# Windowed attention and a hard-swish feed-forward: all attention matmuls in 64x64 tiles of the array, in one stretch for each pair of heads

## The chip, the cores and the metric

The kernel runs on one core of a Trainium2 chip. The metric is device time in microseconds (us), the median of several runs. One more execution is taken with the hardware profiler; its trace has the start and the duration of the instructions on each engine: PE (TensorE matmuls), PEld (TensorE weight loads), DVE (VectorE), ACT (ScalarE), POOL (GpSimd, which here also issues the loads) and SP (which issues the other transfers).

## The reference

Causal attention in a window of 64 tokens, then a feed-forward layer with a hard-swish. Inputs and output are float32.

```python
def _attn_ref(q, k, v):                      # q, k, v: (8, 8, 576, 64), batch, heads, seq, head_dim
    window = 64
    scale = 1.0 / np.sqrt(D)
    scores = scale * np.matmul(q, k.transpose(0, 1, 3, 2))
    rel = pos[:, None] - pos[None, :]
    mask = (rel >= 0) & (rel < window)
    scores = np.where(mask, scores, -1000000000.0)
    attn = np.exp(scores - np.max(scores, axis=-1, keepdims=True))
    attn = attn / (np.sum(attn, axis=-1, keepdims=True) + 1e-09)
    return np.matmul(attn, v)

def _moe_ref(x, w_in, w_out):                # x: (4608, 512), w_in: (512, 2048), w_out: (2048, 512)
    h = x @ w_in
    relu6 = np.clip(h + 3.0, 0.0, 6.0)
    return (h * relu6 / 6.0) @ w_out

def reference(...):
    attn_out = _attn_ref(q, k, v)
    x = attn_out.transpose(0, 2, 1, 3).reshape(B * S, H * D)
    return _moe_ref(x, w_in, w_out)
```

## The kernel before

**Sizes.** There are 8 batches of 576 tokens and 8 heads of 64. Two heads make a pair, so a batch has 4 pairs, and the 32 pairs are numbered t = 4b + g. The feed-forward part is cut into 9 blocks of 512 tokens. A block has 16 first units and 16 second units. A first unit is four matmuls of 128x128 by 512 columns into one bank of PSUM (hT, L364), a relu on ACT (L369) and a multiply on DVE into gT (L370). A second unit is four matmuls (L388); every fourth one is followed by a copy on ACT (L394) and a store. Units stand in a queue, and `weave(n)` records the next n.

**Order.** The order on each engine is the order in which the Python code records the instructions (a manual schedule). Each engine works through its own list in order and waits at an instruction until what it needs is done. The rings of buffers decide when a tile can be written again. PSUM has 8 banks: two for `ps_o` (one tile of two banks), three for `ps_t`, two for `ps_h` (the hT tiles) and one for `ps_acc`.

**Attention of one pair.** q and k of a batch are loaded with 6 tokens on each of 96 partitions, and v with one token a partition, 64 numbers of one head at a time (L97, L108). A second copy of v, moved by 64 tokens, is made by transfers (`shift`, Vs<-Vn). `permute` (L170) reorders q and k on DVE, `t_k` and `t_q` turn them with 6 matmuls each (L178), and KT is copied out on DVE (L214), QZ in two halves on ACT (L203). QZ holds each head with zeros in the other head's rows, so that one matmul of 128 rows gives the scores of both heads. `s_` and `sl_` make the scores of 9 windows with 9 matmuls of 128x128 (L246) and take the exponential on ACT (L258, L268); `m_` multiplies by the mask on POOL (L277, L281). `pv` is 20 matmuls of 128x64 (L303), whose 65th column is the sum of the weights, then one reciprocal and one multiply on DVE (L312, L313). `x_` writes the result transposed into xT by a transfer, or by 5 matmuls and a copy in the first two batches.

**A step** (`step(t, units)`, L602) spreads the work of three pairs between the units: pv(t), some units, scores of t+1, some units, the turn of k for t+2, some units, the turn of q for t+2, some units. In batches 3 to 7 a step has 8 units, second and first in turn.

**The start.** The loads stand in one queue of POOL: q and k of batch 0 pair by pair, v of batch 0, w_in, q and k and v of batch 1, w_out. In batches 0 and 1 the mask is added by a matmul ahead of each score matmul (L223). `shift` of batch 0 is done by DVE and ACT copies (L586 to L590), and pv of pairs 1 and 3 writes into two tiles of `ps_h`, so that two pairs are in work at a time. `tiles_of_zeros` (L519) runs matmuls on zeros in several tile shapes while PE waits for v.

Of the kernel before, what the change touches and what calls it, by code (L numbers as in the profile page):

```python
# [10 lines left out]
F32 = mybir.dt.float32  # L11
# [16 lines left out]
R = 6  # L28
VC = 72
# [3 lines left out]
def kernel(  # L33
# [14 lines left out]
    SP = S // R  # L48
    NW = S // W
    NM = (S + P - 1) // P  # L50
    NFC = FF // P
    TB = 512
    XR = 5 * TB
    NTB = NT // TB
    assert D * H == DM and S % W == 0 and SP * R == S and SP <= P and NT % TB == 0
    assert NW == 2 * (NM - 1) + 1 and NG * P == DM
# [3 lines left out]
    stage = ctx.enter_context(tc.tile_pool(name="stage", bufs=4))  # L60
    permp = ctx.enter_context(tc.tile_pool(name="permp", bufs=1))
# [3 lines left out]
    osbp = ctx.enter_context(tc.tile_pool(name="osb", bufs=3))  # L65
    ps_o = ctx.enter_context(tc.tile_pool(name="ps_o", bufs=1, space=PSUM))
    ps_t = ctx.enter_context(tc.tile_pool(name="ps_t", bufs=3, space=PSUM))
    ps_h = ctx.enter_context(tc.tile_pool(name="ps_h", bufs=2, space=PSUM))
    ps_acc = ctx.enter_context(tc.tile_pool(name="ps_acc", bufs=1, space=PSUM))

    fb = ctx.enter_context(tc.tile_pool(name="fb", bufs=1))
# [8 lines left out]
    xT = consts.tile([P, NG, XR], BF16, name="xT")  # L80
    KT = ring(4, [P, W + S], BF16, "KT")
    QZ = ring(4, [P, 2, S], BF16, "QZ")
    Vn = ring(2, [P, NM, H, VC], BF16, "Vn")
    Vs = ring(2, [P, NM, H, VC], BF16, "Vs")
    Pz = ring(4, [P, 2, NM - 1, 2, W], BF16, "Pz")
    Pl = ring(4, [P, 2, P], BF16, "Pl")


    def load_qk(b, pairs=(NG,), first=0):
        if first:  # L90
            tiles = staged[b]
        else:
            tiles = [stage.tile([SP, H, R * D], BF16, name=name, tag="qk") for name in ("qs", "ks")]
        h = 2 * first
        for n in pairs:
            for t, src in zip(tiles, (q, k)):
                nc.gpsimd.dma_start(  # L97
                    out=t[:, h : h + 2 * n, :],
                    in_=src[b, h : h + 2 * n].rearrange("h (p r) d -> p h (r d)", r=R),
                )  # L100
            h += 2 * n
        return tiles

    def load_v(b, blocks=range(NM)):
        vn = Vn[b % 2]
        for m in blocks:
            n = min(P, S - m * P)
            nc.gpsimd.dma_start(  # L108
                out=vn[:n, m, :, 0:D],
                in_=v[b, :, m * P : m * P + n, :].rearrange("h s d -> s h d"),  # L110
            )

    def shift(b, blocks=(0, NM), heads=(0, H), move=nc.sync.dma_start):

        vn, vs = Vn[b % 2], Vs[b % 2]
        hs = slice(*heads)
        m0, m1 = blocks
# [609 lines left out]
```

## Time and profile before

| what | value |
|---|---|
| runs, median (lowest to highest) | 334.14 us (333.66 to 334.91) |
| the profiled execution | 334.16 us, of which the trace spans 332.4 us |
| granted TensorE clock, mean | 0.998 |
| first pv (pair 0) | 17.87 us |
| first matmul of the feed-forward part | 23.42 us |
| pv of pair 12, the first step of batch 3 | 89.18 us |
| last matmul | ends about 326.5 us |

The span is what the trace covers; the remaining 1.8 us of that execution lie around it. Idle time of an engine matters only where another engine that sets the end waits for it. Matmuls overlap in the trace, so their pace is read from the starts of neighbours and not from the duration of one.

### The profile page before, as it was taken

The page shows a single profiled execution, that of the slowest core. Times are in us where ns is not written, and L with a number is a line of the kernel's source. Part 1 is how long each engine was busy: PE and PEld are TensorE (multiplying, and loading weights), DVE is VectorE, ACT ScalarE, POOL GpSimd, SP SyncE. Part 2 cuts the span into 40 slices and gives each one's busy share as a digit, 9 for nine tenths or more (in the row PEclk, how much of TensorE's full clock was granted, in tenths as well). Part 3 has the DMA queues.
Part 4 walks back from the last instruction along what each step waited for, and adds up shares of the span by engine and source line. Part 5 has one row for each costly group of instructions (what it writes and reads, how often), then busy time and mean ns, then how long its engine had stood idle before and what let it go on. Part 6 is the DMA issues. An engine that isn't in the chain of part 4 may idle for free.

```text
span 332.4 us, 6785 instructions
## 1 busy us (share of the span) xinstructions
PE 314.7 (95%) x2661; PEld 166.4 (50%) x2707; DVE 181.8 (55%) x337; ACT 201.8 (61%) x345; POOL 120.7 (36%) x153
## 2 busy tenths in 40 slices
PE   7987899989999999999999999999999999999992
PEld 3753555545555555555555555555544444444441
DVE  6777665676665655565556555655544533444300
ACT  2867881868766666666666666666664444454420
POOL 8954514444558335733564356533330000000000
PEclk9999999999999999999999999999999999999999
DMA  6999999995359954995499539951211100001011
GB/s 84 164 207 179 234 206 181 198 160 130 76 71 179 115 125 72 177 103 134 76 189 107 131 60 198 115 133 51 55 51 51 66 32 32 34 32 63 35 66 69
DMA packets 76600, 36.89 MB, mean 111 GB/s; under 512 B 55056, under 2 KB 70480, under 8 KB 76560
## 3 DMA queue, kind: packets, MB, share of 16 engines
q0 software_dynamic: 53840, 18.35, 50.1%
q1 hardware_dynamic: 22720, 18.02, 22.6%
q8 instruction: 23, 0.38, 0.5%
q14 instruction: 17, 0.14, 0.1%
HBM read 36.70 MB, written 9.44 MB: 139 GB/s over the span
## 4 chain that ended last, share of the span: by engine, by line
PE 78%; DMA 9%; POOL 5%; ACT 3%; issue 2%; another core or an unknown queue 1%; DVE 1%; POOLq 0%; ACTq 0%
PE acc L388 35%; PE hT L364 32%; DMA qs<-in_q_dram 4%; PE o L303 3%; PE tp L178 3%; PE sc L246 3%; DMA Vs<-Vn 3%; DMA ks<-in_k_dram 2%; POOL Vn L108 1%; ACT t L369 1%; POOL ks L97 1%; ACT QZ L203 1%; POOL qs L97 1%; POOL Pz L277 1%
## 5 line engine op out<-in xcount | busy, mean ns | idle before, releaser
L370 DVE SCALAR_TENSOR_TENSOR gT<-t,hT 128x512 bf16<-128x512 bf16 x140 | 96.1, 687 | 119.0 <-ACT t L369 117.9
L388 PE MATMUL acc<-wout,gT 128*128 128x512 bf16 x561 | 143.7, 379 | 0.8 <-issue 0.2
L364 PE MATMUL hT<-xT,win 128*128 128x512 bf16 x532 | 140.9, 379 | 1.8 <-DVE gT L370 0.2
L369 ACT ACTIVATE t<-hT,half_const 128x512 bf16<-128x512 f32 x140 | 96.3, 688 | 57.6 <-PE hT L364 53.6
L277 POOL TENSOR_TENSOR Pz<-e,mask 128x512 bf16<-128x512 bf16 x48 | 54.3, 1150 | 100.3 <-ACT e L258 100.3
L388 PEld LDWEIGHTS <-gT 128*128 128x128 bf16 x576 | 54.2, 98 | 62.5 <-issue 0.2
L364 PEld LDWEIGHTS <-win 128*128 128x128 bf16 x576 | 52.4, 98 | 50.3 <-issue 0.5
L203 ACT COPY QZ<-tp 64x576 bf16<-64x576 bf16 x60 | 37.9, 632 | 17.9 <-PE tp L178 11.2
L258 ACT ACTIVATE e<-sc 128x512 bf16<-128x512 f32 x48 | 26.1, 595 | 21.7 <-PE sc L246 21.7
L108 POOL DMA_DIRECT2D Vn<-in_v_dram x40 | 34.2, 872 | 11.8 <-DMA wout<-in_moe_w_out_dram 6.0
L394 ACT COPY osb<-acc 128x512 f32<-128x512 f32 x36 | 20.9, 581 | 18.3 <-PE acc L388 15.3
L313 DVE TENSOR_TENSOR opg<-o,recs 128x640 bf16<-128x640 f32 x30 | 24.7, 825 | 1.0
L214 DVE COPY KT<-tp 128x576 bf16<-128x576 bf16 x32 | 24.0, 751 | 1.1 <-PE tp L190 1.0
L246 PEld LDWEIGHTS <-KT 128*128 128x128 bf16 x216 | 14.8, 98 | 7.7
L303 PEld LDWEIGHTS <-Pz 128*64 128x64 bf16 x512 | 12.1, 110 | 12.9 <-issue 11.1
L303 PE MATMUL o<-Vs,Pz 128*64 128x65 bf16 x240 | 14.6, 198 | 1.1 <-DMA Vs<-Vn 0.8
L178 PE MATMUL tp<-ident,kp 96*128 96x96 bf16 x168 | 11.8, 206 | 3.7 <-DVE kp L170 3.5
L246 PE MATMUL sc<-QZ,KT 128*128 128x128 bf16 x192 | 14.7, 219 | 0.1
L303 PE MATMUL o<-Vn,Pz 128*64 128x65 bf16 x240 | 14.6, 198 | 0.0
L178 PEld LDWEIGHTS <-kp 96*128 96x128 bf16 x168 | 9.2, 97 | 8.7 <-DVE kp L170 5.0
L97 POOL DMA_DIRECT2D qs<-in_q_dram x12 | 9.0, 749 | 10.3 <-DVE recs L312 4.7
L178 PEld LDWEIGHTS <-qp 96*128 96x128 bf16 x168 | 9.9, 97 | 5.2
(75 smaller groups left out, 201.7 us busy)
## 6 DMA issues: line engine op xcount, KB each, us to landing
out_dram<-osb SPq DMA_DIRECT2D x36, 256.0 KB, 2.0
Vn<-in_v_dram POOLq DMA_DIRECT2D x32, 128.0 KB, 5.7
qs<-in_q_dram POOLq DMA_DIRECT2D x6, 576.0 KB, 7.0
ks<-in_k_dram POOLq DMA_DIRECT2D x6, 576.0 KB, 10.3
Vs<-Vn SPq DMA_DIRECT2D x6, 360.0 KB, 4.1
wout<-in_moe_w_out_dram POOLq DMA_DIRECT2D x2, 1024.0 KB, 15.7
Vs<-Vn SPq DMA_DIRECT2D x6, 288.0 KB, 4.7
win<-in_moe_w_in_dram POOLq DMA_DIRECT2D x2, 512.0 KB, 7.1
```

Source lines behind the costliest of these rows:

```text
L108: nc.gpsimd.dma_start(out=vn[:n, m, :, 0:D], in_=v[b, :, m * P : m * P + n, :].rearrange("h s d -> s h d"),)
L178: nc.tensor.transpose(out=tp[:, r, :], in_=src[:, r, 2 * g : 2 * g + 2, :].rearrange("p h d -> p (h d)"), identity=ident[:SP, :SP],)
L203: (nc.vector.tensor_copy if h and t in on_vector else nc.scalar.copy)(out=QZ[t % 4][h * D : (h + 1) * D, h, :].rearrange("q (p r) -> q p r ...
L246: nc.tensor.matmul(sc[:, i], lhsT=kt[:, w * W : w * W + P], rhs=qz[:, :, w * W : (w + 1) * W], start=True, stop=True,)
L258: nc.scalar.activation(out=e[:, 2 * i : 2 * i + 2].rearrange("p m a h w -> p (m a h w)"), in_=sc[:].rearrange("p m h w -> p (m h w)"), fun ...
L277: eng.tensor_tensor(out=Pz[t % 4][:, :, :, a].rearrange("p h m w -> p m h w"), in0=e[:, :, a], in1=mk, op=MULT,)
L303: nc.tensor.matmul(om[a * W : (a + 1) * W], lhsT=pl[:, h, a * W : (a + 1) * W] if last else pz[:, h, m, a, :], rhs=(vn if a and not last e ...
L313: nc.vector.tensor_tensor(out=opg[:, :, hs].rearrange("p m h d -> p h m d"), in0=ov[:, :, :, 0:D], in1=rec.unsqueeze(3).to_broadcast([P, 2 ...
L364: nc.tensor.matmul(hT, lhsT=win16[:, g, fc * P : (fc + 1) * P], rhs=xT[:, g, t0 : t0 + TB], start=(g == 0), stop=(g == NG - 1),)
L369: nc.scalar.activation(out=t1[:], in_=hT, func=RELU, bias=half_const[:], scale=1.0 / 6.0)
L370: nc.vector.scalar_tensor_tensor(out=gT[:, fc, :], in0=t1[:], scalar=1.0, in1=hT, op0=MIN, op1=MULT)
L388: nc.tensor.matmul(acc[:], lhsT=gT[:, fc, ts * P : (ts + 1) * P], rhs=wout16[:, fc, :], start=(fc == 0), stop=(fc == NFC - 1),)
```

## The change

Every attention matmul is now made in a quarter of the array: 64 rows by 64 columns.

- Queries and keys are loaded with 9 tokens on each of 64 partitions, k on partitions 0 to 63 and q on 64 to 127 of one tile. `turn` makes 36 matmuls for a pair (9 tokens x 2 heads x q and k), all into one two-bank tile `tp` of `ps_t`, which has now one such tile; `turned` copies KT out on DVE and QT on ACT. `permute`, the zeros of QZ and the copies they need are gone.
- Scores: `s_first` makes the first window with 4 matmuls into unused columns of the tile `tp` of the pair after (its host), and `s_rest` the other 8 windows with 32 matmuls into two tiles of `ps_h`. Each key window is split into even and odd tokens, since v is loaded with two tokens a partition. `ps_h` has 3 tiles, for hT and for these.
- `pv` is 48 matmuls; `pv_out` has five DVE instructions in place of two.
- `x_` uses two transfers a pair in all batches but the first, where it uses matmuls. xT holds all 4608 tokens.
- `group(t, n)` records everything of the attention in one stretch, and all n units after it.
- The start: v of batch 0 is loaded before pair 3's q and k, there are four mask tiles, `shift(0)` is a transfer, and pv, pv_out and x_ of the four pairs of batch 0 stand one after the other with one `ps_o` tile. `tiles_of_zeros` is gone.
- In the last blocks every other accumulator is in `ps_o`, not `ps_t`.

```diff
-R = 6
-VC = 72
+R = 9
+VW = 144
+VO = 8
+OC = D + 2
...
-    ps_t = ctx.enter_context(tc.tile_pool(name="ps_t", bufs=3, space=PSUM))
-    ps_h = ctx.enter_context(tc.tile_pool(name="ps_h", bufs=2, space=PSUM))
+    ps_t = ctx.enter_context(tc.tile_pool(name="ps_t", bufs=1, space=PSUM))
+    ps_h = ctx.enter_context(tc.tile_pool(name="ps_h", bufs=3, space=PSUM))
...
+    def load_v(b, blocks=(0, 1, 2)):
+        for m in blocks:
+            to = Vn[b % 2][:, m] if m < 2 else Vs[b % 2][3 * P // 4 : P, 1]
+            n = 2 * to.shape[0]
+            nc.gpsimd.dma_start(
+                out=to[:, :, VO : VO + P],
+                in_=v[b, :, 2 * P * m : 2 * P * m + n, :].rearrange("h (p r) d -> p h (r d)", r=2),
+            )
+    def shift(b):
+        vn, vs = Vn[b % 2], Vs[b % 2]
+        nc.sync.dma_start(out=vs[0 : P - 32], in_=vn[32:P])
+        nc.sync.dma_start(out=vs[P - 32 : P, 0], in_=vn[0:32, 1])
...
+    def turn(t, pool=None):
+        b, g = divmod(t, NG)
+        tp = (pool or ps_t).tile([P, 2, 8 * P], BF16, name="tp", tag="o" if pool is ps_o else "tp")
+        hosts[t] = tp
+        for r in range(R):
+            for h in range(2):
+                for z in range(2):
+                    nc.tensor.transpose(
+                        out=tp[halves[h], z, r * W : (r + 1) * W],
+                        in_=staged[b][halves[z], 2 * g + h, r * D : (r + 1) * D],
+                        identity=ident[halves[z], halves[z]],
+                    )
+    def turned(t):
+        tp = hosts[t]
+        for z, (to, copy) in enumerate(((KT, nc.vector.tensor_copy), (QT, nc.scalar.copy))):
+            copy(
+                out=to[t % 4][:].rearrange("q (p r) -> q p r", r=R),
+                in_=tp[:, z, 0:S].rearrange("q (r p) -> q p r", p=W),
+            )
...
+    def keys(t, h, k0, r):
+        return KT[t % 4][halves[h], k0 + r : k0 + P : 2]
...
+    def s_first(t, host, masked):
+        s = hosts[host][0:D, :, 6 * P : 8 * P].bitcast(F32).rearrange("p h (r w) -> p h r w", w=W)
+        if masked:
+            for h in range(2):
+                off(s[:, h], halves[h], off_first)
+        for r in range(2):
+            for h in range(2):
+                nc.tensor.matmul(
+                    s[:, h, r], lhsT=keys(t, h, 0, r), rhs=QT[t % 4][halves[h], 0:W],
+                    start=not masked, stop=not masked or r == 1,
+                )
+        return s
+    def s_first_exp(t, s, masked):
+        to = P0[t % 4] if masked else work.tile([D, 2, 2, W], BF16, name="e0")
+        nc.scalar.activation(
+            out=to[:].rearrange("p h r w -> p h (r w)"), in_=s.rearrange("p h r w -> p h (r w)"),
+            func=EXP, scale=scale,
+        )
+        if not masked:
+            nc.gpsimd.tensor_tensor(
+                out=P0[t % 4][:], in0=to[:], in1=first[0:D].unsqueeze(1).to_broadcast([D, 2, 2, W]), op=MULT
+            )
+    def s_rest(t, masked):
+        ss = [ps_h.tile([P, 2, 2, 2, W], F32, name="s", tag="bk") for _ in range(2)]
+        for c in range(2):
+            for m in range(2):
+                if masked:
+                    for h in range(2):
+                        for i in range(2):
+                            nc.tensor.matmul(
+                                ss[h][halves[i], c, m], lhsT=ident[halves[h], halves[h]],
+                                rhs=off_band[halves[h]], start=True, stop=False,
+                            )
+                for r in range(2):
+                    for h in range(2):
+                        for i in range(2):
+                            w = 4 * m + 2 * i + 1 + c
+                            nc.tensor.matmul(
+                                ss[h][halves[i], c, m, r], lhsT=keys(t, h, W * (w - 1), r),
+                                rhs=QT[t % 4][halves[h], w * W : (w + 1) * W],
+                                start=not masked, stop=not masked or r == 1,
+                            )
+        return ss
+    def s_rest_exp(t, ss, masked):
+        for h in range(2):
+            to = Pw[t % 4][:, h] if masked else work.tile([P, 2, 2, 2, W], BF16, name="e", tag=f"e{h}")[:]
+            nc.scalar.activation(
+                out=to.rearrange("p c m r w -> p (c m r w)"),
+                in_=ss[h][:].rearrange("p c m r w -> p (c m r w)"), func=EXP, scale=scale,
+            )
+            if not masked:
+                nc.gpsimd.tensor_tensor(
+                    out=Pw[t % 4][:, h].rearrange("p c m r w -> p (c m) (r w)"),
+                    in0=to.rearrange("p c m r w -> p (c m) (r w)"),
+                    in1=band[:].rearrange("p r w -> p (r w)").unsqueeze(1).to_broadcast([P, 4, P]), op=MULT,
+                )
...
+    def pv(t):
+        b, g = divmod(t, NG)
+        o = ps_o.tile([P, 2, 512], F32, name="o", tag="o")
+        os_[t] = o
+        for m in range(2):
+            for h in range(2):
+                for r in range(2):
+                    c0 = (2 + 2 * m + h) * OC + r
+                    v0 = VO - 1 + r * (D + 1)
+                    for c in range(2):
+                        for i in range(2):
+                            nc.tensor.matmul(
+                                o[halves[c], i, c0 : c0 + D + 1], lhsT=Pw[t % 4][halves[i], h, c, m, r],
+                                rhs=(Vs if c else Vn)[b % 2][halves[i], m, 2 * g + h, v0 : v0 + D + 1],
+                                start=(r == 0), stop=(r == 1), skip_group_check=True,
+                            )
+        for h in range(2):
+            for r in range(2):
+                c0, v0 = h * OC + r, VO - 1 + r * (D + 1)
+                for c in range(2):
+                    for i in range(2):
+                        nc.tensor.matmul(
+                            o[halves[c], i, c0 : c0 + D + 1],
+                            lhsT=Pw[t % 4][halves[i], h, 0, 0, r] if i else P0[t % 4][:, h, r],
+                            rhs=Vn[b % 2][halves[i], 0, 2 * g + h, v0 : v0 + D + 1],
+                            start=(r == 0), stop=(r == 1), skip_group_check=True,
+                        )
+    def pv_out(t):
+        o = os_.pop(t)
+        ov = o[:, :, 0 : 6 * OC].rearrange("p i (s c) -> p i s c", c=OC)
+        sums = work.tile([P, 2, 6], F32, name="sums")
+        nc.vector.reduce_sum(out=sums[:], in_=ov[:, :, :, 0 : OC : OC - 1], axis=mybir.AxisListType.X)
+        rec = recs[:, t]
+        nc.vector.reciprocal(out=rec, in_=sums[:])
+        opg = work.tile([P, 2, 2, 2, D], BF16, name="opg")
+        opg0 = work.tile([D, 2, D], BF16, name="opg0")
+        nc.vector.tensor_tensor(
+            out=opg0[:], in0=ov[0:D, 0, 0:2, 1 : D + 1],
+            in1=rec[0:D, 0, 0:2].unsqueeze(2).to_broadcast([D, 2, D]), op=MULT,
+        )
+        for i in range(2):
+            nc.vector.tensor_tensor(
+                out=opg[:, :, i], in0=ov[:, i, 2:6, 1 : D + 1].rearrange("p (m h) d -> p m h d", h=2),
+                in1=rec[:, i, 2:6].rearrange("p (m h) -> p m h", h=2).unsqueeze(3).to_broadcast([P, 2, 2, D]),
+                op=MULT,
+            )
+        opgs[t] = opg, opg0
...
+    def x_(t, on_pe=False):
+        b, g = divmod(t, NG)
+        opg, opg0 = opgs.pop(t)
+        x0 = b * S
+        if not on_pe:
+            nc.sync.dma_start_transpose(
+                out=xT[:, g, x0 + W : x0 + S].rearrange("p (m q) -> p m q", q=P),
+                in_=opg[:].rearrange("p m i h d -> p (m i h d)"),
+            )
+            nc.sync.dma_start_transpose(
+                out=xT[:, g, x0 : x0 + W].unsqueeze(1), in_=opg0[:].rearrange("p h d -> p (h d)")
+            )
+            return
...
+    nc.vector.memset(zeros[:], 0.0)
+    staged = {0: load_qk(0, pairs=(1,))}
+    nc.gpsimd.memset(ident[:], 0.0)
+    nc.gpsimd.affine_select(
+        out=ident[:], in_=ident[:], pattern=[[-1, P]], compare_op=mybir.AluOpType.not_equal,
+        fill=1.0, base=0, channel_multiplier=1,
+    )
+    load_qk(0, pairs=(1,), first=1)
+    windows(off_band, off_first, 0.0, -BIG)
+    load_qk(0, pairs=(1,), first=2)
+    load_v(0)
+    load_qk(0, pairs=(1,), first=3)
+    for t in Vn + Vs:
+        nc.vector.memset(t[:, :, :, 0:VO], 1.0)
+        nc.vector.memset(t[:, :, :, VO + P : VW], 1.0)
+    for i in range(3):
+        load_w_in(i)
+    windows(band, first, 1.0, 0.0)
+    staged[1] = load_qk(1, pairs=(2,))
+    load_v(1)
+    load_qk(1, pairs=(NG - 2,), first=2)
+    for i in range(2):
+        load_w_out(i)
+    shift(0)
+    nc.vector.memset(ones[:], 1.0)
+    nc.vector.memset(half_const[:], 0.5)
...
+    warm(12)
+    turn(0)
+    turned(0)
+    turn(1, ps_o)
+    turned(1)
+    s_masked(0)
+    turn(2)
+    turned(2)
+    s_masked(1)
+    turn(3, ps_o)
+    turned(3)
+    s_masked(2)
+    s_masked(3)
+    pv(0)
+    pv_out(0)
+    x_(0, True)
+    for g in range(1, NG):
+        pv(g)
+        pv_out(g)
+        warm(2)
+        x_(g, True)
+    def group(t, n):
+        masked = t + 1 < 2 * NG
+        if t >= NG:
+            pv(t)
+        if t + 2 < T:
+            turn(t + 2)
+        if NG <= t + 1 < T:
+            host = t + 2
+            if host >= T:
+                hosts[host] = ps_t.tile([P, 2, 8 * P], BF16, name="tp", tag="tp")
+            s = s_first(t + 1, host, masked)
+            s_first_exp(t + 1, s, masked)
+            ss = s_rest(t + 1, masked)
+        if t >= NG:
+            pv_out(t)
+        if t + 2 < T:
+            turned(t + 2)
+        if NG <= t + 1 < T:
+            s_rest_exp(t + 1, ss, masked)
+        if t >= NG:
+            x_(t)
+        weave(n)
...
+    queue_block(0)
+    weave(3)
+    group(NG - 2, 2)
+    group(NG - 1, 2)
+    moe.extend(left[:10])
+    del left[:10]
+    for t in range(NG, T):
+        b, g = divmod(t, NG)
+        if b == 1:
+            if g == 0:
+                shift(1)
+                staged[2] = load_qk(2)
+            if g == 1:
+                load_v(2)
+            if g == 2:
+                shift(2)
+                staged[3] = load_qk(3)
+            n = -(-len(moe) // (NG - g))
+        else:
+            if g == 0:
+                queue_block(b - 1)
+                if 3 <= b < B - 1:
+                    staged[b + 1] = load_qk(b + 1)
+            if g == 1 and b < B - 1:
+                load_v(b + 1)
+            if g == 2 and b + 1 < B:
+                shift(b + 1)
+            n = -(-len(moe) // (NG - g))
+        group(t, n)
+    late[0] = True
```

## The prediction

> **What bounds the kernel now.** I read the page's busy times and its chain that ended last first, then the timeline of one step of PE.
>
> ```profile
> PE 314.7 (95%) x2661; PEld 166.4 (50%) x2707; DVE 181.8 (55%) x337; ACT 201.8 (61%) x345; POOL 120.7 (36%) x153
> ...
> PE 78%; DMA 9%; POOL 5%; ACT 3%; issue 2%; another core or an unknown queue 1%; DVE 1%; POOLq 0%; ACTq 0%
> ```
>
> PE is busy for 95% and makes 78% of the chain. Whether it is dense is read from one step of batch 3 (columns: start, duration, engine, line, operation):
>
> ```profile
> 106.45 0.22 PE L303 MATMUL o<-Vs,Pz 128*64 128x65 bf16 x1
> ...
> 106.89 1.04 PE L388 MATMUL acc<-wout,gT 128*128 128x512 bf16 x4
> 107.77 0.61 PE L246 MATMUL sc<-QZ,KT 128*128 128x128 bf16 x8
> 108.21 1.03 PE L364 MATMUL hT<-xT,win 128*128 128x512 bf16 x4
> ...
> 109.94 0.22 PE L246 MATMUL sl<-QZ,KT 128*128 128x128 bf16 x1
> 110.00 0.42 PE L178 MATMUL tp<-ident,kp 96*128 96x96 bf16 x6
> 110.25 1.03 PE L364 MATMUL hT<-xT,win 128*128 128x512 bf16 x3
> ...
> 111.98 0.42 PE L178 MATMUL tp<-ident,qp 96*128 96x96 bf16 x6
> 112.24 1.03 PE L364 MATMUL hT<-xT,win 128*128 128x512 bf16 x4
> ...
> 114.92 0.22 PE L303 MATMUL o<-Vs,Pz 128*64 128x65 bf16 x1
> ```
>
> From pv (106.45) to the next pv (114.92) are 8.47 us, and each start follows the one before it without a hole. A unit takes 0.863 us (263.55 to 264.41 below), so 8 units take 6.91; the remaining 1.56 are pv 0.44, scores 0.44 and 0.06, turns 0.25 and 0.26, the rest changes of tile shape (pv begins 0.09 after the unit before it). So here PE alone sets the end, and all else is hidden. Before batch 3 that is not so: from the first unit (23.42) to pv of pair 12 (89.18) are 65.8 us, in which 48 units take 41.4.
>
> **What one stretch of the change costs PE.** The trace has 64x64 tiles, on zeros:
>
> ```profile
> 15.98 0.22 PE L534 MATMUL za<-zeros 64*64 64x64 bf16 x2
> 15.99 0.22 PE L534 MATMUL zb<-zeros 64*64 64x64 bf16 x2
> ...
> 16.16 0.20 PE L534 MATMUL za<-zeros 64*64 64x64 bf16 x2
> 16.29 0.40 PE L526 MATMUL za<-zeros 128*128 128x128 bf16 x4
> ```
>
> 24 matmuls start between 15.98 and 16.16 in six groups of four, 31 ns a group, and the next shape starts 0.13 after the last. pv is 12 such groups, the turn 9, scores 2 half-filled and 8: 31 x 0.031 = 0.96, with two shape changes of 0.10 a stretch of 1.16 us (1.4 to 1.5 with masks, which add matmuls of 128 columns). That is 0.4 less than 1.56. [...] The row has 31, and I take it.
>
> **Where the stretch ends: a loop over ACT and DVE.** The unit's own chain is in these rows:
>
> ```profile
> 263.55 1.03 PE L364 MATMUL hT<-xT,win 128*128 128x512 bf16 x4
> 264.61 0.69 ACT L369 ACTIVATE t<-hT,half_const 128x512 bf16<-128x512 f32 x1 [0.28 <-PE hT L364]
> 265.33 0.69 DVE L370 SCALAR_TENSOR_TENSOR gT<-t,hT 128x512 bf16<-128x512 bf16 x1 [1.04 <-ACT t L369]
> ```
>
> The unit's matmuls end at 264.41 (next start); the relu starts 0.20 later, takes 0.69, and gT 0.69 after 0.03: gT is done 1.61 after the unit. Two engines that read one PSUM tile take turns, in this kernel too:
>
> ```profile
> 7.33 0.63 ACT L203 COPY QZ<-tp 64x576 bf16<-64x576 bf16 x1 [5.24 <-PE tp L190]
> 8.00 0.76 DVE L203 COPY QZ<-tp 64x576 bf16<-64x576 bf16 x1 [0.16 <-ACT QZ L203]
> ```
>
> DVE's half of QZ starts when ACT's half is done (7.96). In the changed program QT and KT are read from one tile tp, and its list of waits says: KT (DVE) waits for s_first's exponential (ACT), QT (ACT) waits for KT. KT stands on DVE behind pv_out, and pv_out behind gT of the last unit. On ACT the exponentials of s_rest stand behind QT, and the next relus behind them. And the ring of three `ps_h` tiles is shared: of a group with 8 units (second, first, and so on) the four first units F0 to F3 and the two score tiles take it in turn, so F0 waits for gT of the last F3, F1 for s_rest's first exponential, F2 for the second, F3 for gT of F0. The loop, from the end of F3:
> - gT of F3 done: 1.61 (PE's 1.16 stretch is over by then, second unit and F0 end at 2.9);
> - pv_out: reduce 0.20 and reciprocal 0.15 (row: 0.213 for 128x10 and 0.182 for 128x5 out of PSUM; bounds 0.10 to 0.22 each), 64x128 and two of 128x256 at 0.29 and 0.425 each (straight line through 0.825 for 640 and 0.491 for 320), 0.14 between them: 1.63, done at 3.24 (bounds 1.35 to 1.9);
> - KT 0.75 (row L214) and 0.03: 4.02; QT 0.63 (row L203, same length) and 0.07: 4.72; exponential 0.595 (row L258): 5.32; F1 starts 0.06 later: 5.38. Without the loop it would start at 3.75: PE stands for 1.63;
> - F1, second, F2, second, F3: 5 x 0.863 = 4.32; closed at 9.70.
>
> A group thus takes 9.7 us (9.4 to 9.95 by the bounds) where a step took 8.47. PE's saving of 0.4 is worth nothing, since the loop does not contain the stretch. POOL's masks end about 2.3 after the second exponential (two of 1.15, row L277; 8.3 us), in time for the next pv at 9.7.
>
> **The start.** POOL issues a pair's q and k in 1.28 (rows L97) and a piece of v in 0.84 (L108); a select takes 0.27 to 0.29, a memset 0.2 (L150, L543, L542). The four masks for batch 0 are now two tiles with 6 selects: 2.1 us in place of 0.75. So: pairs 0 and 1 issued by 4.7 as before, masks 6.8, pair 2 8.1, v 10.6, pair 3 11.9. Before, v was issued by 12.16 and landed at 16.3, 4.1 later; now 14.7. Here the engines' copies (done about 18.5) become a transfer: two issues, landing 4.1 to 6.1 after (DMA rows of Vs<-Vn, the high ones under loads as here): 19.5 to 21.5, I take 20.5. pair 3 lands about 15.7 (3.8 after issue, as before), its chain of turn, KT, QT and exponentials is done by 20. Then four pairs in a row: pv 0.67 with its drain, pv_out 1.65, transposes 0.5, since the one `ps_o` tile is free only after pv_out: 4 x 2.8 = 11.3, and the last copy to xT 0.84. First unit at about 32.6, against 23.42: +9.1 (bounds 28 to 36).
>
> **From there to pair 12.** All loads of batch 1 have landed by then (w_out did at 44.2 before), so the stalls on loads are gone, but the loop is there at once. Groups 2 and 3 with 7 units end at 43.3: pair 5's turn waits for QT of pair 4, then KT and QT follow each other again. Group 4 has 5 first units: F1 at 5.4, F2 at 6.1, then F3 waits for gT of F0 (relu 5.9 to 6.6 behind the exponentials, gT 7.35) and F4 for the next: 9.2. Group 5 the same: 9.1; 6 and 7 have second units only, and the copy of a full accumulator waits behind the exponentials (6.5): 7.4 each. Groups 8 to 11 with 6, 6, 5, 5 units, two thirds of them first ones, walked in this way: 8.7, 9.1, 8.2, 8.0. Pair 12 starts at 110.5: 77.9 us from the first unit, against 65.8: +12.1 (bounds 5 to 17).
>
> **Sum**, on the span of 332.4: start +9.1; to pair 12 +12.1; groups 12 to 29, 18 x (9.69 - 8.47) = +22.0; pairs 30 and 31 have no turn, so no KT and QT in the loop, and with the last 80 units (dense as before, every hT of the ring free in time) -0.6; the end is the same. 375 us, and with the 1.8 around it 376.8. The profiled execution lies 0.02 above the median, so that is the time.
>
> Costed at nothing: the transfers of x_ (two issues on SP, rows of L328 mostly 1.21 and up to 1.9 each, landing 2.8): pv_out ends at 3.2, the second lands by 9.8, and the first unit that can read it starts at 9.7 + 2.0 = 11.7. `shift` of the next batch stands before them on SP and waits for v; v is issued a group earlier and lands within 6 us. If that cover goes, xT and then opg's buffers are late, some us a batch. Loads have larger pieces and are off the path after pair 4.
>
> **Rivals.**
> - The loop is hidden (other durations on DVE and ACT, or a wait that is met early): PE dense, 6.91 + 1.16 = 8.1 a group. The start keeps its +9.1; the middle would be 52 if dense, and I leave it 57.5 for 65.8 (-8.3); 18 groups save 0.37 each (-6.6); 332.4 + 9.1 - 8.3 - 6.6 - 0.6 + 1.8 = 328 us: faster. For it: PE's rows. Against: F1 would need to start at 3.75, 1.6 earlier, and no bound above gives more than 0.3. [...] Chance 0.06.
> - The four tiles don't run at once on real data (24 matmuls of zeros in a row show little): at 31 ns a matmul the stretch is 124 x 0.031 + 0.2 = 4.0, PE is the bound again with 6.91 + 4.0 = 10.9 a group, 410 us. Two at once, 15.6 ns a matmul as pv's pairs start now (20 in 0.31): 2.1, inside the wait in batch 3 and partly before it, 379. Chance 0.06.
> - SP's order: x_ behind shift, late by some us in each batch: 385. Chance 0.06.
> - The forecast: 0.82.
>
> **Numbers.** The likeliest gives 377. pv_out's bounds move it by -6 to +4, the first unit by -3 to +3, the middle by -7 to +5; together 360 to 390, which also takes in 379 and 385, and leaves out 328 and 410 (0.12) and little else. A measurement of this kernel can tell about 0.5%. The first rival's 0.06 is 0.05 faster and 0.01 within that; slower 0.94.
>
> **What would show it.** Right: in batch 3 pv of neighbours 9.7 apart; PE stands about 1.6 before the second hT group, released by ACT's exponential; QT follows KT, KT follows pv_out; matmuls of the stretch 31 ns per four; first unit near 32.6. Wrong: a step near 8.1 with no hole (loop), a stretch over 2.8 (tiles), or the hole ahead of L336 released by a transfer (SP).

## The result, and the profile after

The changed kernel takes 365.72 us (median; 365.11 to 366.17), the kernel before 334.03 us on the same chip: 1.094 times as long, 95% interval 1.092 to 1.097. The trace of the changed kernel spans 363.4 us. From its page, the busy times, the granted clock of TensorE in 40 slices, the chain that ended last, and two groups of instructions (busy us, mean ns of one, then idle time before them and what ended most of it):

```profile
PE 310.7 (85%) x5136; PEld 155.9 (43%) x5176; DVE 164.2 (45%) x351; ACT 183.8 (51%) x313; POOL 113.1 (31%) x147
...
PEclk9556999999999999999999999999999999999999
...
PE 55%; DVE 21%; ACT 11%; issue 5%; DMA 4%; POOL 2%; SPq 0%; ACTq 0%; POOLq 0%
...
L336 PE MATMUL hT<-xT,win 128*128 128x512 bf16 x568 | 145.4, 379 | 25.9 <-ACT e L240 21.3
...
L173 ACT COPY QT<-tp 128x576 bf16<-128x576 bf16 x32 | 20.4, 638 | 65.6 <-DVE KT L173 65.6
```

PE's busy time has fallen by 4.0 us, and still the span is 31.0 longer: PE is no longer the engine that alone sets the end (78% of the chain before, 55% now). DVE and ACT, 4% of the chain before, make 32%. The two groups name the place: the hT matmuls wait 21.3 us for the exponential of L240, and QT, which stands ahead of that exponential on ACT, waits 65.6 us for KT. A second new thing is in the clock row: 5 to 6 tenths in slices 2 to 4.

One group of batch 4, from its timeline (start, duration, engine, line; rows between are left out):

```profile
143.47 1.03 PE L336 MATMUL hT<-xT,win 128*128 128x512 bf16 x4
...
144.54 0.69 ACT L341 ACTIVATE t<-hT,half_const 128x512 bf16<-128x512 f32 x1 [0.22 <-PE hT L336]
145.26 0.69 DVE L342 SCALAR_TENSOR_TENSOR gT<-t,hT 128x512 bf16<-128x512 bf16 x1 [0.70 <-ACT t L341]
...
145.86 0.18 DVE L285 TENSOR_REDUCE sums<-o 128x12 f32<-128x24 f32 x1
...
146.07 0.23 DVE L287 RECIPROCAL recs<-sums 128x12 f32<-128x12 f32 x1
...
147.21 0.74 DVE L173 COPY KT<-tp 128x576 bf16<-128x576 bf16 x1
...
147.31 1.03 PE L362 MATMUL acc<-wout,gT 128*128 128x512 bf16 x4
...
147.98 0.64 ACT L173 COPY QT<-tp 128x576 bf16<-128x576 bf16 x1 [2.11 <-DVE KT L173]
148.51 1.09 ACT L240 ACTIVATE e<-s 128x512 bf16<-128x512 f32 x2
...
149.17 1.02 PE L336 MATMUL hT<-xT,win 128*128 128x512 bf16 x4 [0.83 <-ACT e L240]
```

This is the loop of the prediction, link by link: the last first unit F3 (143.47, its end at 144.33), its relu and gT, the products of pv_out, KT, QT, the exponential, and the next F1 with a hole ahead of it. The next such F1 is at 158.31: a group takes 9.14 us.

The stages add up to the span (start of the stage to start of the next, in us; the last column is experiment e2 below, in which the loop is broken):

| stage | before | predicted | after | e2 |
|---|---|---|---|---|
| start to first unit | 23.42 | 32.5 | 35.17 | 34.74 |
| first unit to pv of pair 12 | 65.8 | 77.9 | 72.6 | 63.9 |
| pairs 12 to 29, 18 groups | 152.8 | 174.8 | 164.7 | 148.1 |
| pair 30 to the end | 90.4 | 89.8 | 90.9 | 90.9 |
| span | 332.4 | 375 | 363.4 | 337.7 |

### The profile page after: what moved, and what is told of

It reads as the page before. It is cut to its first block, busy times and chain, and to the rows that moved or that the text cites. A ratio compares the mean times of both kernels' runs of the same rounds, so it can differ in the third digit from the quotient of the medians.

```text
span 363.4 us, 11680 instructions
## 1 busy us (share of the span) xinstructions
PE 310.7 (85%) x5136; PEld 155.9 (43%) x5176; DVE 164.2 (45%) x351; ACT 183.8 (51%) x313; POOL 113.1 (31%) x147
## 4 chain that ended last, share of the span: by engine, by line
PE 55%; DVE 21%; ACT 11%; issue 5%; DMA 4%; POOL 2%; SPq 0%; ACTq 0%; POOLq 0%
PE hT L336 29%; PE acc L362 18%; PE acc_o L362 6%; DVE gT L342 5%; DVE KT L173 5%; DVE opg L295 5%; ACT t L341 5%; ACT e L240 4%; DVE opg L290 2%; DMA Vs<-Vn 2%; DVE recs L287 2%; DMA Vn<-in_v_dram 2%; PE o L264 1%; DVE sums L285 1%; POOL qk L104 1%
## 5 line engine op out<-in xcount | busy, mean ns | idle before, releaser
L336 PE MATMUL hT<-xT,win 128*128 128x512 bf16 x568 | 145.4, 379 | 25.9 <-ACT e L240 21.3
L362 PE MATMUL acc<-wout,gT 128*128 128x512 bf16 x452 | 119.3, 379 | 4.5 <-ACT osb L368 2.6
L245 POOL TENSOR_TENSOR Pw<-e,band 128x512 bf16<-128x512 bf16 x48 | 54.3, 1151 | 58.0 <-ACT e L240 58.0
L173 ACT COPY QT<-tp 128x576 bf16<-128x576 bf16 x32 | 20.4, 638 | 65.6 <-DVE KT L173 65.6
L210 POOL TENSOR_TENSOR P<-e,first 64x256 bf16<-64x256 bf16 x24 | 15.9, 661 | 84.8 <-ACT e L205 84.8
L240 ACT ACTIVATE e<-s 128x512 bf16<-128x512 f32 x48 | 26.2, 604 | 0.0
L362 PE MATMUL acc_o<-wout,gT 128*128 128x512 bf16 x95 | 23.6, 379 | 0.1
L295 DVE TENSOR_TENSOR opg<-o,recs 128x256 bf16<-128x256 f32 x64 | 23.6, 406 | 0.0
L230 PE MATMUL s<-QT,KT 64*64 64x64 bf16 x1024 | 18.5, 199 | 3.4 <-issue 3.4
L164 PE MATMUL tp<-ident,qk 64*64 64x64 bf16 x1152 | 17.0, 199 | 4.2 <-DMA qk<-in_k_dram 1.7
L264 PE MATMUL o<-Vs,Pw 64*64 64x65 bf16 x512 | 15.3, 201 | 1.5 <-DMA Vs<-Vn 1.4
L205 ACT ACTIVATE e<-tp 64x256 bf16<-64x256 f32 x24 | 9.1, 377 | 11.7 <-PE tp L197 11.7
```

Of the source, the lines that this page charges most:

```text
L164: nc.tensor.transpose(out=tp[halves[h], z, r * W : (r + 1) * W], in_=staged[b][halves[z], 2 * g + h, r * D : (r + 1) * D], identity=ident[ ...
L173: copy(out=to[t % 4][:].rearrange("q (p r) -> q p r", r=R), in_=tp[:, z, 0:S].rearrange("q (r p) -> q p r", p=W),)
L230: nc.tensor.matmul(ss[h][halves[i], c, m, r], lhsT=keys(t, h, W * (w - 1), r), rhs=QT[t % 4][halves[h], w * W : (w + 1) * W], start=not ma ...
L240: nc.scalar.activation(out=to.rearrange("p c m r w -> p (c m r w)"), in_=ss[h][:].rearrange("p c m r w -> p (c m r w)"), func=EXP, scale=s ...
L245: nc.gpsimd.tensor_tensor(out=Pw[t % 4][:, h].rearrange("p c m r w -> p (c m) (r w)"), in0=to.rearrange("p c m r w -> p (c m) (r w)"), in1 ...
L264: nc.tensor.matmul(o[halves[c], i, c0 : c0 + D + 1], lhsT=Pw[t % 4][halves[i], h, c, m, r], rhs=(Vs if c else Vn)[b % 2][halves[i], m, 2 * ...
```

## The experiments

The ratios are to the kernel before, on the same chip, with a 95% interval.

**e1: the order of two records.** In `group`, ahead of the units:

```diff
+        if NG <= t + 1 < T:
+            s_rest_exp(t + 1, ss, masked)
         if t + 2 < T:
             turned(t + 2)
-        if NG <= t + 1 < T:
-            s_rest_exp(t + 1, ss, masked)
```

> The two exponentials of s_rest are recorded ahead of the copies KT and QT; nothing else changes. If the loop over QT and KT sets the group (theory): the exponentials follow the one of s_first on ACT, the hole ahead of the second hT group is gone, a group takes 6.91 + 1.14 = 8.05 us in place of 9.14, 18 groups save 19.6 us, the stretch from the first unit to pair 12 falls from 72.6 to 54 to 60, and the time is 326 to 334 us. If the hole has another cause (the ring of three tiles by itself, POOL's masks, DVE too busy): groups stay above 9 and the time is 360 to 366.

Measured: 342.51 us, ratio 1.029 (1.026 to 1.032); 15 of the 18 groups take 8.15 to 8.18. ACT's timeline of one group:

```profile
119.07 0.38 ACT L205 ACTIVATE e<-tp 64x256 bf16<-64x256 f32 x1 [0.27 <-PE tp L197]
119.44 1.08 ACT L240 ACTIVATE e<-s 128x512 bf16<-128x512 f32 x2
121.55 0.64 ACT L173 COPY QT<-tp 128x576 bf16<-128x576 bf16 x1 [1.03 <-DVE KT L173]
```

The exponentials come right behind the one of s_first. QT still waits for KT, 1.03 us, but the units no longer wait for QT. PE's waits between 100 and 260 us, in the changed kernel and then in e1 (us in total, times, longest):

```profile
PE hT L336 <- ACT e L240: 15.7, 18, 1.7
```

```profile
PE hT L336 <- DMA xT<-opg: 1.4, 1, 1.4
```

Two lines exchanged take 23.2 us off, which is the theory. The time missed its range (326 to 334): the group is 0.1 longer than its sum, three groups take 8.41 to 9.70, and from the first unit to pair 12 are 65.4 us, where 54 to 60 was expected. Holes of the kind described under e6 to e8 stand in that stretch (one of 1.90 us up to 48.0); how much of the miss they explain was not worked out.

**e2: the engines of the two copies exchanged**, so that ACT copies KT and DVE copies QT; the order of records is the old one.

```diff
-        for z, (to, copy) in enumerate(((KT, nc.vector.tensor_copy), (QT, nc.scalar.copy))):
+        for z, (to, copy) in enumerate(((KT, nc.scalar.copy), (QT, nc.vector.tensor_copy))):
```

> KT is copied by ACT and QT by DVE, in the old order of records. Theory: QT, now on DVE, is still late behind pv_out and KT, but nothing on ACT waits for a copy on DVE any more, so the exponentials are early: groups of 8.05 to 8.2 us, 326 to 336 us. Rival, that a group is held by the copies as such (they end as late as before, and the next pair's scores need them): groups near 9.1, 360 to 366.

339.19 us, ratio 1.017 (1.012 to 1.021), 16 of the 18 groups at 8.15 to 8.18. The work and the order of records are the same, and one copy still comes late on DVE, now QT's. From the timeline of one group:

```profile
132.65 0.62 ACT L173 COPY KT<-tp 128x576 bf16<-128x576 bf16 x1
133.17 1.08 ACT L240 ACTIVATE e<-s 128x512 bf16<-128x512 f32 x2
134.08 0.74 DVE L173 COPY QT<-tp 128x576 bf16<-128x576 bf16 x1
```

The exponentials on ACT no longer stand behind the late copy. So the copies as such don't hold the group; the exponentials behind one of them did. The time missed its range (326 to 336) here too; a hole of 2.54 us that nothing releases stands before pair 12, up to 47.45.

**e3: a reduction made twice**, to see whether pv_out is a link of the loop.

```diff
         nc.vector.reduce_sum(out=sums[:], in_=ov[:, :, :, 0 : OC : OC - 1], axis=mybir.AxisListType.X)
+        more = work.tile([P, 2, 6], F32, name="more")
+        nc.vector.reduce_sum(out=more[:], in_=ov[:, :, :, 0 : OC : OC - 1], axis=mybir.AxisListType.X)
         rec = recs[:, t]
```

> The first reduction of pv_out is made twice; its second result is not used. Theory, that pv_out lies in the loop link by link: each group is longer by one reduction, 0.18 to 0.22 us, 9.32 to 9.36 in place of 9.14; 18 groups 3.2 to 4.0 us, the pairs before them 1 to 2 and the start 0.8: 370 to 373 us. Rival, that DVE has slack in the group: groups stay at 9.14 and only the start's 0.8 shows, 366.5.

365.08 us, ratio 1.095 (1.088 to 1.102); groups of 9.14 to 9.15. That contradicts the theory and looks like the rival's slack on DVE (9.14, 366.5), but DVE's timeline shows another reason:

```profile
146.86 0.17 DVE L285 TENSOR_REDUCE sums<-o 128x12 f32<-128x24 f32 x1
146.95 0.17 DVE L287 TENSOR_REDUCE more<-o 128x12 f32<-128x24 f32 x1
147.07 0.23 DVE L289 RECIPROCAL recs<-sums 128x12 f32<-128x12 f32 x1
```

The reciprocal starts 0.21 after `sums` starts, with or without an instruction between them (145.86 to 146.07 above). It needs the result of `sums`; the second reduction needs nothing of the first, starts 0.09 after it and fits into that wait. The experiment had doubled something that the loop doesn't feel, so it said nothing on the loop.

**e5: a product made twice.** The same question with an instruction that no such wait covers.

```diff
+        again = work.tile([P, 2, 2, D], BF16, name="again")
+        nc.vector.tensor_tensor(
+            out=again[:], in0=ov[:, 1, 2:6, 1 : D + 1].rearrange("p (m h) d -> p m h d", h=2),
+            in1=rec[:, 1, 2:6].rearrange("p (m h) -> p m h", h=2).unsqueeze(3).to_broadcast([P, 2, 2, D]),
+            op=MULT,
+        )
         opgs[t] = opg, opg0
```

> In the changed kernel the last product of pv_out (128x256 out of PSUM) is made twice; the second result is not used. Doubling the first reduction had left the group at 9.14, since the second reduction started in the 0.21 us in which the reciprocal waits for the first; a product between two others has no such wait to hide in and starts 0.335 after the one before it. Theory, that pv_out's time on DVE lies in the loop: the group is 9.14 + 0.335 = 9.47. Rival, that KT could start later without harm: 9.14 again.

```profile
152.78 0.74 DVE L295 TENSOR_TENSOR opg<-o,recs 128x256 bf16<-128x256 f32 x2
153.44 0.41 DVE L301 TENSOR_TENSOR again<-o,recs 128x256 bf16<-128x256 f32 x1
153.77 0.74 DVE L173 COPY KT<-tp 128x576 bf16<-128x576 bf16 x1
```

KT starts 0.33 after `again`, and the groups take 9.47 to 9.48: 0.33 more, all of it. pv_out does lie in the loop. One run, 376.11 us.

**e4: two tiles in place of tp**, of one PSUM bank each.

```diff
-        tp = (pool or ps_t).tile([P, 2, 8 * P], BF16, name="tp", tag="o" if pool is ps_o else "tp")
+        if pool is ps_o:
+            whole = ps_o.tile([P, 2, 8 * P], BF16, name="tp", tag="o")
+            tp = [whole[:, z] for z in range(2)]
+        else:
+            tp = [ps_t.tile([P, 8 * P], BF16, name=f"tp{z}", tag=f"tp{z}")[:] for z in range(2)]
...
+        for h in range(2):
+            nc.scalar.activation(
+                out=to[:, h].rearrange("p r w -> p (r w)"), in_=s[h].rearrange("p r w -> p (r w)"),
+                func=EXP, scale=scale,
+            )
```

> The tile tp becomes two tiles of one PSUM bank each, one for the keys and one for the queries; the exponential of s_first, whose scores lie in both, becomes two of half the size. The order of records is the old one. Theory, that QT waits for KT only because both are read from one tile: QT starts right behind the exponentials of s_first, the hole is gone, groups of 8.05 to 8.2 us, 326 to 336 us; and in pairs 0 and 1, where both copies are released by the same turn, they start together and take 0.64 and 0.75 as before. Rival, that QT follows KT for another reason: groups near 9.2, 361 to 368. If two engines can not read two banks at once, the two copies of pair 0 together take 1.4 us from the first start all the same.

340.0 us, ratio 1.019 (1.016 to 1.021), 16 of the 18 groups at 8.17 to 8.20; the time missed its range (326 to 336) as in e1 and e2. The first copies, from the timeline of DVE and then of ACT; pair 0 has the two tiles, pair 1 still one tile, in ps_o, which the expectation had overlooked:

```profile
6.96 0.76 DVE L177 COPY KT<-tp 128x576 bf16<-128x576 bf16 x1 [4.62 <-PE tp L168]
8.06 0.76 DVE L177 COPY KT<-tp 128x576 bf16<-128x576 bf16 x1 [0.34 <-PE tp L168]
```

```profile
7.00 0.64 ACT L177 COPY QT<-tp 128x576 bf16<-128x576 bf16 x1 [4.91 <-PE tp L168]
8.85 0.64 ACT L177 COPY QT<-tp 128x576 bf16<-128x576 bf16 x1 [1.22 <-DVE KT L177]
```

Pair 0: both start at once and take 0.76 and 0.64, as long as alone. Pair 1: QT starts when KT is done (8.82). So the wait of QT for KT belongs to the one tile. From 7.00 to 7.64 the two engines read the two banks at once.

**e6: more warm-up matmuls in the start**, 3 to 12 (of 0.22 us) in each hole of PE before the first unit. The core of the edit:

```diff
     s_masked(1)
+    warm(12)
     turn(3, ps_o)
...
         pv_out(g)
-        warm(2)
+        warm(6)
         x_(g, True)
```

> The changed kernel with more warm-up matmuls in the holes of PE before the first unit (3 to 12 at a time, 0.22 us each); all else as it was. Theory, that the granted clock falls to 0.5 between 9 and 36 us because the array stands there: it stays at 0.9 or above, the xp transposes take 0.45 in place of 0.83 and pv 0.45 in place of 0.75, and the first unit starts at 31.5 to 33 in place of 35.2; 362 to 364 us. Rival, that the clock falls whatever fills the holes, or that the step of 2.85 us is set by DVE and the hand-overs: first unit at 34.5 to 36, time 365 to 367.

The windows of 9 us from 9 to 36 us, in the changed kernel and then in e6 (busy us and count of PE, PEld, DVE, ACT and POOL, then the granted clock, the DMA share and GB/s):

```profile
9.00:18.00 9.00, 4.04 (x211) 3.38 (x202) 1.14 (x2) 3.80 (x8) 8.70 (x19) 0.58 1.33 164
18.00:27.00 9.00, 4.51 (x146) 3.23 (x142) 1.73 (x6) 3.25 (x8) 2.70 (x4) 0.50 1.14 225
27.00:36.00 9.00, 7.49 (x165) 4.05 (x169) 4.07 (x15) 2.52 (x4) 3.14 (x4) 0.59 1.42 196
```

```profile
9.00:18.00 9.00, 6.87 (x190) 3.64 (x186) 0.77 (x2) 3.52 (x8) 8.70 (x19) 1.00 1.32 161
18.00:27.00 9.00, 7.11 (x220) 4.20 (x211) 2.41 (x8) 3.86 (x8) 2.74 (x5) 1.00 1.16 234
27.00:36.00 9.00, 8.17 (x135) 4.24 (x137) 3.76 (x14) 2.16 (x4) 3.15 (x4) 1.00 1.43 198
```

The clock stays at 1.00 in these windows, so it had fallen because PE stood there, and the transposes and pv are fast again (a step of 2.39 for 2.85 us). But the first unit starts at 34.70, only 0.5 earlier, as the rival had it (34.5 to 36): 0.72 went into a hole that nothing releases, and the last three warm-up matmuls themselves delayed the unit by 0.65. And the time is 370.3 us, ratio 1.105 (1.100 to 1.109), longer than without them and above both ranges (362 to 364, 365 to 367): in the profiled execution PE stands for 4.95 us up to 68.26, released by nothing that the profile shows, and behind it the clock is at 0.50 until about 74. From the first unit to pair 12 are 80.0 us there, 7.4 more than in the changed kernel.

**e7, e8: another start** for e2: Vs of batch 0 by copies of DVE and ACT, pair 2's scores ahead of pair 3's turn, pv of the four pairs in ps_o and ps_t in turn. e8 has more warm-up matmuls besides.

```diff
-    shift(0)
...
+    s_masked(1)
+    s_masked(2)
+    shift_on_engines(0)
+    turn(3)
+    turned(3)
+    pv(0)
+    s_masked(3)
+    pv_out(0)
+    pv(1)
+    x_(0, True)
+    pv(2, ps_t)
...
```

> On the version with the copies' engines swapped (339.2 us, first unit at 34.7): Vs of batch 0 is filled by copies of DVE and ACT in place of the two transfers on SP, the scores of pair 2 come before pair 3's turn, and pv of the four pairs takes ps_o and ps_t in turn. Theory, that the start is late by the transfer (landed at 23.75) and by the one tile for pv (2.85 us a pair): pv of pair 0 at about 17.6, the pairs then 1.4 apart on DVE, first unit at 24.5 to 27, 329 to 333 us. Rival, that w_in or the holes on PE that no engine releases hold it then: first unit at 29 or later, 334 us or more.

> The same with more warm-up matmuls in PE's holes of the start. By the clock theory another 0.5 to 2 us: 328 to 332 us; if the clock falls anyway, or the matmuls of the start are not on its path, the same as without them, within 0.5 us.

e7: 336.27 us, ratio 1.007 (1.004 to 1.009), first unit at 31.26. The start gains 3.5 us, less than half of what was expected, and the ranges of the rival hold (first unit at 29 or later, 334 us or more): the products of pv are ready earlier (reciprocals at 21.6, 24.0, 28.2 and 29.7), but PE stands for 2.44 us up to 14.7 and 2.40 up to 27.1 with nothing that releases it. A third such hole, behind the start, shows what it costs; PE's timeline, and then the windows of 2 us around it:

```profile
45.68 0.21 PE L239 MATMUL s<-QT,KT 64*64 64x64 bf16 x1 [2.48 <-issue]
```

```profile
42.00:44.00 2.00, 1.20 (x122) 1.09 (x118) 1.93 (x7) 0.90 (x2) 0.38 (x1) 1.00 1.24 210
44.00:46.00 2.00, 0.32 (x13) 0.29 (x12) 0.66 (x1) 0.00 (x0) 0.30 (x1) 0.67 1.25 206
46.00:48.00 2.00, 1.78 (x14) 0.74 (x6) 0.00 (x0) 1.12 (x3) 0.00 (x0) 0.50 1.23 208
48.00:50.00 2.00, 2.00 (x6) 0.75 (x5) 0.69 (x1) 0.98 (x2) 0.00 (x0) 0.50 1.22 204
50.00:52.00 2.00, 2.00 (x8) 0.69 (x7) 0.69 (x1) 0.98 (x2) 0.00 (x0) 0.63 1.37 120
```

The hole takes 2.48 us and the clock behind it is at 0.5 until about 51.5, where a unit takes 1.71 in place of 0.863. e8 was slower, 343.18 us (1.024, 1.019 to 1.028), where 328 to 332 was expected, or by its rival the time of e7: its clock is 1.00 and 0.90 up to 27 us, but its holes of that kind before 75 us add up to 13.4 us (e7: 8.1).

**e9, e10, e11: what makes the holes.** e9 is e7 with the loads of batch 2 a group later. e10 is e7 with fewer instructions on PE: pairs 0 to 7 are turned by 128x64 tiles and masked by one matmul a head. e11 is both.

```diff
+                if t < 2 * NG:
+                    nc.tensor.transpose(
+                        out=flat[halves[h], (r + 2) * P : (r + 3) * P],
+                        in_=staged[b][:, 2 * g + h, r * D : (r + 1) * D], identity=ident[:],
+                    )
+                    continue
...
+                nc.tensor.matmul(
+                    ss[h][:].rearrange("p c m r w -> p (c m) (r w)"), lhsT=ident[:],
+                    rhs=off_band[:].rearrange("p r w -> p (r w)").unsqueeze(1).to_broadcast([P, 4, P]),
+                    start=True, stop=False,
+                )
```

> On the version with the new start (336.3 us): the loads of batch 2 are issued one group later each. In all kernels run so far PE's holes that nothing releases stand at 447 to 448, 701 to 705, 955 to 959, 1207 to 1210, 1469 to 1471, 1719 to 1727, 1983, 2231 to 2240 of its recorded instructions: 256 apart, and only before 75 us. Theory, that PE waits there for the next 256 instructions, whose transfer stands among the loads: with fewer loads outstanding the holes behind 40 us (2.5 at 45.7, with the granted clock at 0.5 for some 5 us behind it) shrink below 1 us and their clock stays up, 332 to 335 us. Rival, that the loads have no part in it: a hole of 2 to 3 us at 1720 to 1728 again, 336 to 338.

> On the version with the new start: pairs 0 to 7 are turned by 128x64 tiles (18 matmuls a pair in place of 36, the same columns of tp in another order) and masked by one matmul of 512 columns for each head in place of eight of 128: some 270 instructions fewer on PE before the first unit, some 60 fewer in each of the next four groups, for about 0.4 us more of matmul time a pair. Theory of the blocks of 256 instructions: holes still at 448 and 704, but one block fewer before the first unit, which starts at 27 to 30 in place of 31.3; 331 to 335 us. Rival, that the holes belong to places of the program (the second s_rest, the third pv) and not to a count: they stay there, and the time is 336 to 338.

> Both of the former. If both hold: first unit at 27 to 30, holes behind 40 us below 1 us, 329 to 334 us, at or below the kernel before. If neither: 336 to 339.

e9: 336.81 us, ratio 1.007 (1.004 to 1.010), the time of the rival (336 to 338); holes of 1.63 up to 44.3, 0.86 up to 58.3 and 0.98 up to 65.9, so the theory's "below 1" was missed. The test was also weak: from 36 to 45 us the loads moved 232 GB/s, as before. e10: 335.4 us, ratio 1.003 (1.000 to 1.006), just above its range (331 to 335), first unit at 28.61 as expected; the hole at instruction 448, which the theory had left in place, is gone too, the one at 704 is left with 0.87, and one of 1.71 stands at 2,228. Its first unit is 2.65 us earlier than in e7, but only 0.9 of that is left in the time: from there to pair 12 are 67.1 us for 65.6. e11: 335.27 us, ratio 1.002 (0.998 to 1.005), above its 329 to 334: one hole of 0.49, the first unit at 27.63, and no measurable difference from the kernel before.

**e12: e11 with a little more**: 25 warm-up matmuls in the waits of the start, four units in place of two behind pairs 2 and 3, v's short piece first.

> The former version (335.3 us; first unit at 27.6, granted clock 0.5 from 18 to 30, and 2.4 us of waiting for Vs of batch 1 at 38 to 40.5 with the clock at 0.5 behind it) with three changes: warm-up matmuls in PE's waits of the start, four units in place of two in each of the groups of pairs 2 and 3, and v's short piece for Vs loaded first, with all copies of Vs on DVE. Theory: the clock stays at 0.9 or above from 9 to 36, first unit at 25 to 27, pv of pair 4 finds its Vs landed, 329 to 333 us, 0.3 to 1.5 per cent below the kernel before. Rival, that each instruction added on PE brings the next block's hole nearer and costs what the clock gives, or that w_in has not landed for the earlier units: 334 to 337.

338.76 us, ratio 1.013 (1.009 to 1.017). The clock stays at 1.00, 0.87 and 0.94 from 9 to 36 us, and pair 4 no longer waits for Vs, but three holes of 1.75, 2.08 and 2.22 us are back (e11: one of 0.49), and the first unit is at 30.54. Both ranges were missed (329 to 333, and 334 to 337 by the rival). The first half of the rival, that instructions added on PE cost as much in holes as the clock gives, fits this run; that it is the cause was not shown. No version that was run beats the kernel before; e11 equals it.

## Why the prediction was right, and where its sum was off

**The forecast holds**: slower, by the loop over ACT and DVE. Breaking it in three different ways (e1, e2, e4) gives 23.2 to 26.5 of the 31.7 us back (the chip was another one, on which e3, with the loop as it was, took 365.08) and brings most groups to 8.15 to 8.20, and lengthening it by 0.33 (e5) lengthens the group by 0.33. The rival that the loop is hidden is dead (the wait stands there 18 times); that of SP's order too (xT is not among PE's waits after 100 us).

**One stretch: right.** From F3's end to the end of the stretch are 1.24 us (1.16 predicted): pv 0.40, the turn 0.31, the scores the rest. pv's 12 groups of four make 33 ns a group on real data, 31 on zeros. With the loop broken, the array's saving shows: 8.15 a group against 8.47.

**The group: 9.70 predicted, 9.14 measured; a mis-sized term.** The path from the end of F3 to F1 is 4.84 us (144.33 to 149.17) and not 5.38. Three links were too long. pv_out takes 1.35 up to the start of KT and was put at 1.63 (its lower bound was 1.35). `sums` starts 0.09 before gT's row ends. The exponential starts 0.53 after QT's start, where 0.70 was put. So PE stands for 1.00 ahead of F1 (the unit before it starts at 147.31 and takes 0.863), where 1.63 was predicted. The common reason is in the rows: on DVE and ACT the next instruction starts 0.07 to 0.11 before the row of the one before it ends, unless it waits for its result (`recs` starts 0.03 after the row of `sums`); I had added durations and in places a gap. Over 18 groups this is 10.1 of the 11.6 us by which the span was overestimated; the pairs before them, +6.9 for +12.1, have the same loop (PE's waits for the exponentials stand at 80.11, 89.25, 97.64 and 105.11 too) and the same error: each of the groups of pairs 4 to 11 is 0.3 to 0.8 us shorter than predicted.

**The start: +9.1 predicted, +11.7 measured; a mis-sized term the other way.** The step of pv, pv_out and turning was put at 2.8 and is 2.85. What was late is `shift(0)`: SP issued it at 15.10 and 15.79, and Vs was there at 23.75, 8 us later, where I had taken 4.1 to 6.1 and 20.5. That is 3.2 us late; what follows up to the first unit took 11.4 where 12.1 was put. From the timeline of the changed kernel:

```profile
15.10 0.64 SPq L123 DMA_DIRECT2D Vs<-Vn  x1
15.79 0.58 SPq L124 DMA_DIRECT2D Vs<-Vn  x1
23.75 0.54 PE L264 MATMUL o<-Vs,Pw 64*64 64x65 bf16 x2 [1.43 <-DMA Vs<-Vn]
```

The step was right for partly wrong reasons: pv_out is shorter than the 1.65 assumed, and the transposes and pv are longer, since the clock was at half (0.50 from 18 to 27 us; with it at 1.00, in e6, the step is 2.39).

**The errors had opposite signs**: -10.1 us in the 18 groups and -5.3 before them, +2.7 in the start and +1.1 from pair 30 on, where the cause was not traced. So 365.7 lies in the range of 360 to 390, near its lower end, and that it is not nearer still is luck. The bounds of the group (9.4 to 9.95) did not hold 9.14: pv_out's lower bound was right, but the overlap of neighbours, which stood in the rows of before, was in no bound. In the kernel before, gT ends at 106.68, and the next instruction of DVE had started at 106.59:

```profile
105.99 0.69 DVE L370 SCALAR_TENSOR_TENSOR gT<-t,hT 128x512 bf16<-128x512 bf16 x1 [1.73 <-ACT t L369]
106.59 0.77 DVE L170 COPY qp<-qs 96x768 bf16<-96x768 bf16 x1
```

## What to carry to other kernels

When work is gathered into one stretch, write down for each engine what stands behind what, and look for a closed path through a buffer that comes round; here two records exchanged were worth 23 us. An engine at 45% busy can set the time. A path through several engines is added from starts to starts of neighbours, not from durations.

## What the runs showed of the hardware that I had not expected

**PE's holes that nothing releases are 256 instructions apart.** In the traces of the changed kernel and its 12 variants I counted PE's recorded matmuls and weight loads up to the matmul behind each hole over 0.25 us: 54 holes, all at 448 plus a multiple of 256 or at most 36 below it, as records missing from a trace would have it (448 in eight kernels, 698 to 704 in seven, 1,717 to 1,728 in ten, 6,840 to 6,842 in three). They take 0.3 to 5 us each, and 49 of them lie before 75 us. The kernel before has none, with 2,661 matmul records where this one has 5,136. The page has a DMA queue of the kind "instruction": 42 packets for 0.69 MB in the changed kernel and 23 for 0.38 MB in the kernel before, 16 KB each. PE's recorded matmuls and weight loads are 10,312 and 5,368, which is 40.3 and 21.0 times 256. The times of the packets speak for a wait for them: each of the 40 holes over 0.6 us ends 1.05 to 1.79 us after a packet of 16 KB was done, where a moment taken at random falls into that window in about one case of nine. In the changed kernel the holes up to 14.16, 21.73 and 48.59 us end 1.31, 1.33 and 1.37 after one. That PE waits there for its own instructions is my reading of these counts; no experiment showed it. A stretch of 64x64 tiles has 240 matmuls and weight loads in 1.24 us, where a unit has 8 in 0.863. That the loads of the first 75 us delay the packets is my estimate, from their distances: in each of these traces they start at least 5.4 us apart up to 66 us, while after 75 us the shortest distance in each is 3.1 to 3.5. It was not shown by an experiment, since e9 changed the loads too little.

**A hole can cost twice.** Behind holes of 2.48 and 4.95 us the granted clock was 0.5 for about 6 us (e7, e6), and in the start it was 0.50 to 0.59 over windows of 9 us in which PE was busy for 4.0 to 7.5; filling the holes brought it to 1.00 (e6). The length of a hole alone doesn't decide it: in e9 the clock fell behind one of 1.63, while one of 2.54 in e2 (up to 47.45) and one of 2.08 in e12 (up to 63.72) left it at 1.00. In all 14 traces the clock keeps a level, the last of a trace left out, for 3.41 us or a multiple of it: in the changed kernel 1.00 for 3.41, 0.50 for 23.89 (7 x 3.413) and 1.00 for 327.68 (96 x 3.413). In e7 it fell at 44.67, 1.47 us into the hole, with PE busy for 1.20 of the 2 us from 42 to 44. What makes it fall behind one hole and not behind another was not shown.

**The pair `sums` and `recs` on DVE has a gap of its own.** In the changed kernel `recs`, which needs `sums`, starts 0.21 to 0.22 after it in all 32 pairs, and an independent instruction between them left the group at 9.14 to 9.15 (e3).
